# Sums of q for batch 4 added up on GpSimd, and seven products that begin ahead of their mixes, in an attention and MLP kernel

## The chip, the cores and the metric

The kernel runs on one core of a Trainium2 chip. The metric is the device time of the whole program in microseconds (us). The engines are named as the profile names them: PE is TensorE, DVE is VectorE, ACT is ScalarE, POOL is GpSimd, and SP is the engine whose queue issues most of the DMAs.

## The reference, cut to what matters

There are 8 batches of 8 heads, 576 tokens and 64 dimensions per head, and an MLP of width 2048 behind the attention.

```python
q_lm = q.reshape(B, H, m, S // m, D).mean(axis=3)      # m = 32 landmarks, 18 tokens each
k_lm = k.reshape(B, H, m, S // m, D).mean(axis=3)
A  = sm(q, k_lm); Bm = sm(q_lm, k_lm); C = sm(q_lm, k)
Z  = Bm.transpose(0, 1, 3, 2) / (norm1(Bm) * norminf(Bm) + 1e-06)
for _ in range(6):
    Z = 2 * Z - Z @ Bm @ Z
x = A @ Z @ C @ v                                       # heads side by side: 576 x 512 per batch
xn = (x - mean) / sqrt(var + 1e-06) * g_ln
out = x + maximum(xn @ w_ch1, 0) @ w_ch2
```

The landmarks are means over 18 tokens. The kernel works with sums in their place and puts the division into the scale of the exponentials. A tile of q or k holds four heads of a batch; each of its 128 partitions holds nine consecutive tokens of two heads (`[128, 2, 9, 64]`), so a landmark is the sum over the nine slots of a partition and over two neighbouring partitions.

## The kernel before, in words

The batches run as a pipeline in the sets (0), (1), (2), (3, 4), (5, 6) and (7). Class `Coming` (L971) prepares a set: `next_load` issues the loads, `next_cast` turns each tile to fp16 (`cast`, L1105), `next_job` runs the DVE steps (a transposition `turn`, and a step that brings the sums into landmark form), and `attention2` (L1263) follows. In a set of two batches the tiles are k0, k1, q0, q1 of the first batch, then k2, k3, q2, q3 of the second.

The nine slots are summed in one of three ways, picked for each tile where `sets` is built (L1848): on DVE (`add_up`, reductions of the transposed tile), on POOL right behind the cast (four additions of 512, 256, 128 and 128 columns, L1130 to L1138, into a small tile `s16` that DVE turns in `turn_sums`), or on PE (`total`, L1043). `total` runs nine products against the constant `pairs16`, which adds neighbouring partitions and spreads the result over the rows; the nine add up in one PSUM bank. ACT copies it to `tot`, and `turn_totals` turns that on DVE into the tile `lm` of landmarks. In set (3, 4), k0 and k1 go by DVE, q0 and q1 by POOL, and k2, k3, q2, q3 (batch 4) by PE.

A cast runs on POOL, or on ACT if, at the moment it is placed, the kernel's own clock says that POOL is busy and ACT is free (`helps`, L1913).

For each batch the attention ends with `normalize` (L653): PE sums the heads (`psd`), ACT takes logarithm and exponential (`lns`), POOL multiplies `ea` by it. The batch's rows (`zcbd` by `ea`, into x) and the first MLP layer (`chunk`, L1564: `psh` from `m16` and `ea`) both read the normalized `ea`. ReLU, mostly on ACT, writes the hidden tile `hT`.

The second MLP layer multiplies `hT` by `w2_16`. For batches 4 to 7 it is `seven_products` (L1738), a Strassen form for a 512 x 512 block: seven products in place of eight, of mixed operands. The mixes of the weights (`w2mix`, t1 to t4) are made once by POOL (`mix_w2`), those of the hidden tile (s1, s2 and the rewritten h21) for each batch by DVE (`mix_ahead`). The first two products, h11 by w11 and h12 by w21, read no mixes. As the code stands, the generator first waits until all mixes of the batch are placed, and then begins with those two.

All engines execute in program order. This order is written out by hand in `ORDER` (L1853): a list of letters and counts that says which stream places its next step. 0 is the attentions, 1 the totals, 2 the first layers, 4 the second layers, J a DVE job, M a measurement of a block, X a mix of the hidden tile, W one of the weights, K a cast, L a load. A step that isn't possible at its turn is placed as soon as it is. Changing one entry can change every queue behind it.

Of the kernel before, what the change touches and what calls it, by code (L numbers as in the profile page):

```python
# [16 lines left out]
P = 128  # L17
# [3 lines left out]
def kernel(  # L21
# [20 lines left out]
    MCH = HID // P  # L42
    U = H // 4
    NJ = 9
# [17 lines left out]
    NEVER = 1e12  # L62
# [4 lines left out]
    parted, mixed_, parted_w1 = {}, set(), set()  # L67
# [219 lines left out]
    clock = Clock()  # L287
# [245 lines left out]
    asm = Ring(name="asm", bufs=2)  # L533
# [435 lines left out]
                    block_done(j)  # L969

    class Coming:  # L971
        def __init__(self, bs, by_dve, by_pe=()):
            self.bs, self.by_dve, self.by_pe = bs, by_dve, by_pe
            self.units = [(b, u) for b in bs for u in range(U)]
            pairs = [(w, w + 1) for w in range(0, len(self.units), 2)]
            self.parts = [(nm, w) for pair in pairs for nm in ("k", "q") for w in pair]
            self.parts += [("v", w) for w in range(len(self.units))]
            n = len(self.units)
            self.loads, self.casts = list(range(3 * n)), list(range(3 * n))
            self.jobs = []  # L980
            for i, (nm, w) in enumerate(self.parts[:2 * n]):
                self.jobs.append((self.turn, i))
                if nm + str(w) in by_pe:
                    self.jobs.append((self.turn_totals, i))
                elif nm + str(w) in by_dve:
                    self.jobs += [(self.add_up, i, 0), (self.add_up, i, 1)]
                else:
                    self.jobs.append((self.turn_sums, i))
            self.stg, self.n16, self.sums, self.xT, self.part, self.lm = {}, {}, {}, {}, {}, {}
            self.totals, self.uses, self.lm_tiles = {}, {}, {}  # L990
# [14 lines left out]
        def cast_ready(self):  # L1005
            i = self.casts[0]
            if i not in self.stg:
                return NEVER
            nm, w = self.parts[i]
            if nm == "v":  # L1010
                b = self.units[w][0]
                if b - 2 not in multiplied:
                    return NEVER
                return max(clock.at(self.stg[i]), clock.idle(natv_buf[b % NV]))
            return max(clock.at(self.stg[i]), nat.next("nat"),
                       asm.next("s16") if self.by_pool(nm, w) else 0.0)

        def by_pool(self, nm, w):
            return nm + str(w) not in self.by_dve and nm + str(w) not in self.by_pe
# [13 lines left out]

        def total_ready(self, i):
            if self.bs not in PAIRED:
                if i not in self.n16:
                    return NEVER
                return max(clock.at(self.n16[i]), banks.next(), asm.next("tot"))
            if i not in self.n16 or i + 1 not in self.n16:
                return NEVER  # L1040
            return max(clock.at(self.n16[i], self.n16[i + 1]), banks.next(2), asm.next("tot", 2))

        def total(self, i):  # L1043

            if self.bs not in PAIRED:
                psl = banks.take([P, 2, D])
                for j in range(NJ):
                    MM(psl, pairs16[:].rearrange("p e h l -> p (e h l)"), self.n16[i][:, :, j, :],
                       start=(j == 0), stop=(j == NJ - 1))
                self.totals[i] = asm.pin(asm.tile([P, 2, D], FP16, name="tot", tag="tot", bufs=4 if PAIRED else 2))  # L1050
                scalar.copy(self.totals[i][:], psl)
                self.used(i)
                return
            psl = [banks.take([P, 2, D]) for _ in range(2)]
            for j in range(NJ):
                for x in range(2):
                    for e in range(2):
                        rows, cb = ds(64 * e, 64), 64 * (e ^ x)
                        MM(psl[x][ds(cb, 64)], pairs16[rows, e, :, :].rearrange("p h l -> p (h l)"),
                           self.n16[i + x][rows, :, j, :], rb=64 * e, cb=cb,  # L1060
                           start=(j == 0), stop=(j == NJ - 1), skip=True)
            for x in range(2):
                t = asm.pin(asm.tile([P, 2, D], FP16, name="tot", tag="tot", bufs=4))
                self.totals[i + x] = t
                for to, of in (((slice(0, P), slice(0, P)),) if x == 0 else
                               ((slice(0, 64), slice(64, P)), (slice(64, P), slice(0, 64)))):
                    scalar.copy(t[to], psl[x][of])
                self.used(i + x)
# [36 lines left out]
        def cast(self, i, by_act=False, part=None):  # L1105
# [19 lines left out]
            else:  # L1125
                pool.tensor_copy(out=t[:], in_=stg[:])
            self.n16[i] = nat.pin(t)
            self.uses[i] = 2 if nm + str(w) in self.by_pe else 1
            if self.by_pool(nm, w):
                s = asum.tile([P, 2, 4, D], FP32, name="asum", tag="asum")  # L1130
                s16 = asm.tile([P, 2, D], FP16, name="s16", tag="s16", bufs=4)
                self.sums[i] = asm.pin(s16)
                for o, x, y in ((s[:], t[:, :, 0:4, :], t[:, :, 4:8, :]),
                                (s[:, :, 0:2, :], s[:, :, 0:2, :], s[:, :, 2:4, :]),
                                (s[:, :, 0, :], s[:, :, 0, :], s[:, :, 1, :]),
                                (s16[:], s[:, :, 0, :], t[:, :, 8, :])):
                    with nc.allow_low_precision("sums are rounded once, to fp16"):
                        pool.tensor_tensor(out=o, in0=x, in1=y, op=ALU.add)  # L1138
# [597 lines left out]
            h_mixed.add(b)  # L1736

    def seven_products(b):  # L1738

        while b not in h_mixed:  # L1740
            yield lambda: NEVER if b not in h_mixed and len(w2_mix) < 6 else 0.0
            if b not in h_mixed:
                if hTs[b].name not in mixed_:
                    yield lambda: clock.at_key(hTs[b][:, MCH - 1, 0:P])
                mix_ahead()
        t1, t2, t3, t4, s1, s2 = [t[:] for t in w2_mix]
        h11, h12, h21, h22 = parts_of(b)
        j0 = 9 * (b // 2) + 4 * (b % 2)

# [35 lines left out]
        yield from finished(b)  # L1785
        if not early:
            add(0, 0, a)
        yield from product(a, s2, t2, False)
        add(0, 0, e)
        banks.release(e[0])  # L1790
# [52 lines left out]
    def scaled_by_pe():  # L1843
# [2 lines left out]
        dve.tensor_scalar(out=g_sb[:], in0=psg[:], scalar1=UP, scalar2=None, op0=ALU.mult)  # L1846

    sets = [Coming((1,), (), ("k0", "k1", "q0", "q1"))]  # L1848
    sets += [Coming(bs, [f"k{w}" for w in range(U * len(bs))] if bs != (3, 4) else ["k0", "k1"], ("k2", "k3", "q2", "q3") if bs == (3, 4) else ()) for bs in ((2,), (3, 4), (5, 6), (7,))]

    begun_first = [0]

    ORDER = (  # L1853
# [19 lines left out]
    ).split()  # L1873
    JOB, MEASURE, CENTER, MIX, MIX_W2, CAST, LOAD, MEANS = range(5, 13)

# [175 lines left out]
```

## Time and profile before

| | us |
|---|---|
| median of 3 runs | 260.68 (260.4 to 261.2) |
| profiled execution, its own time | 260.16 |
| profiled execution, span from first to last instruction | 258.4 |
| PE matmul busy in the span | 250.6 |
| DVE busy | 203.8 |
| ACT busy | 174.0 |
| POOL busy | 141.0, nearly all of it before 166 us |

The page divides the span over 40 slices of 6.46 us. POOL is nearly always at work from slice 4 to slice 25 and rests for most of the last third; ACT is between 4 and 9 tenths busy, DVE mostly 8 or 9. In the chain of work that ended last, PE has 92% of the span. A busy PE isn't a PE at its peak: matmuls overlap in the pipeline, and the profile models their ends. The distance between the starts of two groups in the chain of waits, or in the timeline, says more than the mean duration of one matmul, which also holds the way through the array.

### The profile page before, as it was taken

The numbers are of one execution on the slowest core, as the hardware profiler recorded it, in microseconds if no ns is written. First come the engines' busy times: TensorE is split into PE (matmuls) and PEld (weight loads), VectorE is DVE, ScalarE is ACT, GpSimd is POOL, SyncE is SP. The second block draws the span as 40 slices with busy tenths as digits, with TensorE's granted clock in tenths as the row PEclk, the third lists the DMA queues.
The fourth block names the chain that finished last, engine by engine and source line by source line (L and its number), as shares of the span: only waits on it lengthen the run. The fifth ranks groups of instructions, "written<-read, shape, count | busy, mean of one in ns | idle before, by whom it ended". The sixth has DMA issues, their size and how long they took to land.

```text
span 258.4 us, 8623 instructions
## 1 busy us (share of the span) xinstructions
PE 250.6 (97%) x3551; PEld 168.4 (65%) x3551; DVE 203.8 (79%) x464; ACT 174.0 (67%) x335; POOL 141.0 (55%) x166
## 2 busy tenths in 40 slices
PE   6889999999999999999999999999999999999994
PEld 6645754556455664546655466688878875888883
DVE  2768966999988989997998865968398878697861
ACT  2788976468858986389987668647888737786000
POOL 5188789999992889689899997300000006000000
PEclk9999999999999999999999999999999999999999
DMA  6999999997976895858943101300240034100705
GB/s 252 373 398 371 394 405 393 365 335 235 352 212 185 299 351 157 257 169 225 365 129 79 46 5 40 81 3 1 68 99 1 3 81 94 32 3 3 162 20 186
DMA packets 23119, 46.70 MB, mean 181 GB/s; under 512 B 2980, under 2 KB 3240, under 8 KB 23080
## 3 DMA queue, kind: packets, MB, share of 16 engines
q1 hardware_dynamic: 22600, 45.50, 54.4%
q10 hardware_dynamic: 480, 0.66, 0.8%
q8 instruction: 28, 0.46, 0.7%
q14 instruction: 11, 0.09, 0.1%
HBM read 36.70 MB, written 9.44 MB: 179 GB/s over the span
## 4 chain that ended last, share of the span: by engine, by line
PE 92%; DMA 2%; DVE 2%; POOL 1%; issue 0%; ACT 0%; SPq 0%; DVEq 0%; POOLq 0%
PE bank L345 60%; PE psh L345 25%; DMA stg<-in_q_dram 2%; PE pscv L345 2%; PE psd L345 2%; PE psea L345 1%; PE psec L345 1%; PE psr L345 1%; POOL w L339 1%; PE pszt L345 0%; DVE st L339 0%; SPq L354 0%; DVE m L339 0%; PE pszc L345 0%; DVE nat L339 0%
## 5 line engine op out<-in xcount | busy, mean ns | idle before, releaser
L345 PE MATMUL bank<-w,hT 128*128 128x512 f16 (+3 forms) x528 | 111.6, 335 | 0.0
L339 ACT ACTIVATE hT<-psh 128x576 f16<-128x576 f32 x122 | 76.9, 655 | 26.3 <-PE psh L345 25.1
L345 PE MATMUL psh<-ea,m 128*128 128x288 f16 x512 | 80.6, 286 | 0.3 <-DVE m L339 0.2
L345 PEld LDWEIGHTS <-hT 128*128 128x128 f16 x656 | 60.4, 98 | 28.1 <-issue 4.3
L345 PEld LDWEIGHTS <-m 128*128 128x128 f16 x512 | 49.4, 98 | 19.5 <-issue 0.7
L339 DVE SCALAR_TENSOR_TENSOR xblk<-bank,rstd,xblk 128x256 f32<-128x256 f32 (+2 forms) x77 | 39.0, 539 | 19.4 <-PE bank L345 18.7
L339 POOL TENSOR_TENSOR ea<-ea,lns 128x576 f16<-128x576 f16 x16 | 20.9, 1318 | 55.8 <-ACT lns L339 55.8
L339 POOL CAST nat<-stg 128x1152 f16<-128x1152 f32 x27 | 31.2, 1165 | 9.4 <-DVE xT L339 4.7
L339 DVE BATCH_NORM_STATS2 six<-xblk 128x6 f32<-128x512 f32 x36 | 24.3, 676 | 0.5 <-ACT xblk L339 0.4
L339 POOL CAST natv<-stg 128x1152 f16<-128x1152 f32 (+1 forms) x17 | 19.4, 1165 | 8.5 <-DMA stg<-in_v_dram 8.4
L339 DVE STREAM_TRANSPOSE xT<-nat 128x576 uint32<-128x576 uint32 x28 | 21.2, 758 | 0.0
L339 DVE SCALAR_TENSOR_TENSOR st<-st,bank 128x128 f16<-128x128 f16 (+3 forms) x36 | 13.2, 367 | 8.2 <-PE bank L345 8.0
L339 ACT ACTIVATE lns<-psd 128x576 f32<-128x576 f32 x16 | 10.3, 647 | 11.7 <-PE psd L345 11.6
L345 PE MATMUL bank<-w2mix 128*128 128x256 f16 x128 | 17.8, 273 | 0.0
L345 PE MATMUL bank<-w2mix,hT 128*128 128x256 f16 x128 | 17.2, 273 | 0.0
L339 DVE TENSOR_REDUCE part<-xT 128x32 f16<-128x576 f16 x20 | 14.5, 738 | 0.1
L339 ACT CAST m<-bank 128x512 f16<-128x512 f32 x20 | 11.3, 589 | 4.1 <-PE bank L345 3.9
L339 ACT COPY xblk<-bank 128x512 f32<-128x512 f32 (+1 forms) x22 | 12.9, 598 | 1.2 <-PE bank L345 1.0
L345 PEld LDWEIGHTS <-w2mix 128*128 128x128 f16 x128 | 12.4, 98 | 2.0
L345 PEld LDWEIGHTS <-st 32*32 32x32 f16 (+1 forms) x380 | 7.0, 90 | 9.3 <-DVE st L339 4.3
L339 POOL TENSOR_TENSOR asum<-asum 128x256 f32<-128x256 f32 (+1 forms) x20 | 12.2, 609 | 1.6
L339 ACT ACTIVATE ea<-psea 128x576 f16<-128x576 f32 x14 | 8.3, 648 | 6.9 <-PE psea L345 6.9
(132 smaller groups left out, 370.1 us busy)
## 6 DMA issues: line engine op xcount, KB each, us to landing
stg<-in_q_dram SPq DMA_DIRECT2D x16, 576.0 KB, 6.8
stg<-in_k_dram SPq DMA_DIRECT2D x15, 576.0 KB, 5.2
out_dram<-xblk SPq DMA_DIRECT2D x66, 128.0 KB, 2.4
wstg<-in_moe_w_ch_dram SPq DMA_DIRECT2D x16, 512.0 KB, 7.1
stg<-in_v_dram SPq DMA_DIRECT2D x5, 576.0 KB, 6.9
stg<-in_v_dram SPq DMA_DIRECT2D x40, 72.0 KB, 2.7
stg<-in_v_dram SPq DMA_DIRECT2D x6, 288.0 KB, 5.5
stg<-in_v_dram SPq DMA_DIRECT2D x12, 144.0 KB, 2.9
```

The source lines that it names most:

```text
L339: return lambda *args, **kw: keep(getattr(self.engine, op)(*args, **kw))
L345: keep(nc.tensor.matmul(o, l, r, start=start, stop=stop, tile_position=(rb, cb), skip_group_check=(skip or cb != 0)))
```

## The change

Class `Coming` takes one more list, `added`. A tile in `by_pe` that is also in `added` is cast as before, then summed by POOL with the same four additions as q0 and q1, and `total` multiplies the sum once by `pairs16` in place of the nine slots. The tile's own fp16 copy then has one reader, the transposition, in place of two. The list names q2 and q3 of set (3, 4), the two q tiles of batch 4; k2 and k3 keep their nine products each.

In `seven_products` the loop that waits for the mixes moves from the head of the generator to the place in front of the third product, the first one that reads a mix.

`ORDER` is written anew. The first difference on PE is at about 65 us of the span. From there the order of fillers, casts, jobs, mixes, measurements and loads shifts by a few places, at many places; the kinds and numbers of the instructions stay the same but for those named here and the choice between ACT and DVE, or ACT and POOL, for a few copies.

```diff
-            self.bs, self.by_dve, self.by_pe = bs, by_dve, by_pe
+            self.bs, self.by_dve, self.by_pe, self.added = bs, by_dve, by_pe, added
...
+        def summed(self, nm, w):
+            return self.by_pool(nm, w) or nm + str(w) in self.added
...
             if self.bs not in PAIRED:
+                if i in self.sums:
+                    return max(clock.at(self.sums[i]), banks.next(), asm.next("tot"))
                 if i not in self.n16:
                     return NEVER
...
                 psl = banks.take([P, 2, D])
-                for j in range(NJ):
-                    MM(psl, pairs16[:].rearrange("p e h l -> p (e h l)"), self.n16[i][:, :, j, :],
-                       start=(j == 0), stop=(j == NJ - 1))
+                added = self.sums.pop(i, None)
+                of = ([self.n16[i][:, :, j, :] for j in range(NJ)] if added is None
+                      else [added[:]])
+                for j, x in enumerate(of):
+                    MM(psl, pairs16[:].rearrange("p e h l -> p (e h l)"), x,
+                       start=(j == 0), stop=(j == len(of) - 1))
...
-            self.uses[i] = 2 if nm + str(w) in self.by_pe else 1
-            if self.by_pool(nm, w):
+            self.uses[i] = 2 if nm + str(w) in self.by_pe and nm + str(w) not in self.added else 1
+            if self.summed(nm, w):
...
     def seven_products(b):
-
-        while b not in h_mixed:
-            yield lambda: NEVER if b not in h_mixed and len(w2_mix) < 6 else 0.0
-            if b not in h_mixed:
-                if hTs[b].name not in mixed_:
-                    yield lambda: clock.at_key(hTs[b][:, MCH - 1, 0:P])
-                mix_ahead()
-        t1, t2, t3, t4, s1, s2 = [t[:] for t in w2_mix]
         h11, h12, h21, h22 = parts_of(b)
...
         if not early:
             add(0, 0, a)
+        while b not in h_mixed:
+            yield lambda: NEVER if b not in h_mixed and len(w2_mix) < 6 else 0.0
+            if b not in h_mixed:
+                if hTs[b].name not in mixed_:
+                    yield lambda: clock.at_key(hTs[b][:, MCH - 1, 0:P])
+                mix_ahead()
+        t1, t2, t3, t4, s1, s2 = [t[:] for t in w2_mix]
         yield from product(a, s2, t2, False)
...
+    sets += [Coming(bs, ..., ("k2", "k3", "q2", "q3") if bs == (3, 4) else (),
+                    ("q2", "q3") if bs == (3, 4) else ()) for bs in ((2,), (3, 4), (5, 6), (7,))]
```

More of the change, by code (lines that the diff above doesn't have):

```diff
@@ L971, with __init__ @@
     class Coming:
-        def __init__(self, bs, by_dve, by_pe=()):
-            self.bs, self.by_dve, self.by_pe = bs, by_dve, by_pe
+        def __init__(self, bs, by_dve, by_pe=(), added=()):
+            self.bs, self.by_dve, self.by_pe, self.added = bs, by_dve, by_pe, added
             self.units = [(b, u) for b in bs for u in range(U)]
@@ L1015, in cast_ready @@
             return max(clock.at(self.stg[i]), nat.next("nat"),
-                       asm.next("s16") if self.by_pool(nm, w) else 0.0)
+                       asm.next("s16") if self.summed(nm, w) else 0.0)
+        def summed(self, nm, w):
+            return self.by_pool(nm, w) or nm + str(w) in self.added
         def by_pool(self, nm, w):
@@ L1046, in total @@
                 psl = banks.take([P, 2, D])
-                for j in range(NJ):
-                    MM(psl, pairs16[:].rearrange("p e h l -> p (e h l)"), self.n16[i][:, :, j, :],
-                       start=(j == 0), stop=(j == NJ - 1))
+                added = self.sums.pop(i, None)
[4 more added lines that the diff above has]
+                       start=(j == 0), stop=(j == len(of) - 1))
                 self.totals[i] = asm.pin(asm.tile([P, 2, D], FP16, name="tot", tag="tot", bufs=4 if PAIRED else 2))
                 scalar.copy(self.totals[i][:], psl)
-                self.used(i)
+                if added is None:
+                    self.used(i)
+                else:
+                    asm.unpin(added)
                 return
@@ L1848 @@
     sets = [Coming((1,), (), ("k0", "k1", "q0", "q1"))]
-    sets += [Coming(bs, [f"k{w}" for w in range(U * len(bs))] if bs != (3, 4) else ["k0", "k1"], ("k2", "k3", "q2", "q3") if bs == (3, 4) else ()) for bs in ((2,), (3, 4), (5, 6), (7,))]
+    sets += [Coming(bs, [f"k{w}" for w in range(U * len(bs))] if bs != (3, 4) else ["k0", "k1"], ("k2", "k3", "q2", "q3") if bs == (3, 4) else (),
+                    ("q2", "q3") if bs == (3, 4) else ()) for bs in ((2,), (3, 4), (5, 6), (7,))]
     begun_first = [0]
     ORDER = (
[19 rows of a table removed]
[19 rows of a table added]
     ).split()
```

38 rows, old and new, of the table ORDER are left out of this document.

## The prediction

> **What bounds the kernel now.** I read the page's busy shares first, then the table of stretches, then the chain of waits, and last the timelines of single engines around the places that the change touches.
>
> ```profile
> span 258.4 us, 8623 instructions
> ...
> PE 250.6 (97%) x3551; PEld 168.4 (65%) x3551; DVE 203.8 (79%) x464; ACT 174.0 (67%) x335; POOL 141.0 (55%) x166
> ```
>
> ```profile
> 60.00:76.00 16.00, 16.00 (x218) 9.77 (x217) 14.80 (x37) 12.39 (x26) 15.37 (x17) 1.00 0.80 259
> 76.00:92.00 16.00, 16.00 (x157) 9.53 (x155) 14.67 (x31) 13.62 (x26) 9.99 (x9) 1.00 0.79 246
> ...
> 156.00:172.00 16.00, 16.00 (x202) 11.06 (x201) 11.93 (x24) 10.84 (x20) 6.26 (x6) 1.00 0.16 36
> 172.00:188.00 16.00, 16.00 (x221) 13.06 (x219) 10.44 (x23) 11.62 (x22) 0.00 (x0) 1.00 0.15 35
> ```
>
> The columns are the stretch, its length, then PE, PE's weight loads, DVE, ACT and POOL. PE is busy for 16.00 of 16 us in each stretch shown, and has no gap that the profile would book as a wait. The granted clock is 1.00. So in the middle of the program PE's own queue is the bound: a product taken from it shortens the end by its slot, and each new wait of PE lengthens it by its full length. POOL is nearly full from 60 to 76 us (15.37 of 16), less so from 76 to 92 (9.99): that is where the change adds to POOL.
>
> **The products that go.** In the changed program, 72 products of `nat` by `pairs16` become 54, and 2 of the sums come in: 16 fewer. Nothing else on PE differs in number.
>
> ```profile
> 92.81 0.50 PE bank L345 x9
> ...
> 107.16 1.18 PE pscv L345 x68
> ...
> 150.48 0.65 PE pscv L345 x35
> 151.36 0.65 PE pscv L345 x36
> ```
>
> The first row of the chain of waits is one of the two groups of nine that go: 0.50 / 9 = 0.056 us each, 16 x 0.056 = 0.89 us. The removed weight loads ran beside the products. The last three rows price a second, small gain of the new order: in set (5, 6) the two groups of `pscv` now stand side by side, with the step of the iteration behind them instead of between them. Side by side in set (3, 4), 72 products (4 of them not recorded) took 1.18 us, apart 2 x 0.65 = 1.30, so 0.12 us.
>
> **What POOL and ACT take over.** Four additions more for each of q2 and q3, and two casts (k3 and q2) that go from POOL to ACT.
>
> ```profile
> 65.18 1.54 POOL L339 TENSOR_TENSOR asum<-nat 128x512 f32<-128x512 f16 x1
> 66.80 1.60 POOL L339 TENSOR_TENSOR asum<-asum 128x256 f32<-128x256 f32 x2
> 68.47 0.49 POOL L339 TENSOR_TENSOR s<-asum,nat 128x128 f16<-128x128 f32 x1
> ...
> 70.13 1.16 POOL L339 TENSOR_TENSOR asum<-nat 128x512 f32<-128x512 f16 x1
> 71.37 1.26 POOL L339 TENSOR_TENSOR asum<-asum 128x256 f32<-128x256 f32 x2
> 72.71 0.43 POOL L339 TENSOR_TENSOR s<-asum,nat 128x128 f16<-128x128 f32 x1
> 73.08 1.15 POOL L339 CAST nat<-stg 128x1152 f16<-128x1152 f32 x1
> 74.18 1.29 POOL L339 TENSOR_TENSOR ea<-ea,lns 128x576 f16<-128x576 f16 x1
> 75.41 1.15 POOL L339 CAST nat<-stg 128x1152 f16<-128x1152 f32 x1
> 76.52 1.80 POOL L339 TENSOR_TENSOR ea<-ea,lns 128x576 f16<-128x576 f16 x1
> 82.98 1.14 POOL L339 CAST nat<-stg 128x1152 f16<-128x1152 f32 x1 [4.67 <-DVE xT L339]
> 84.07 4.49 POOL L339 CAST natv<-stg 128x1152 f16<-128x1152 f32 x4
> ```
>
> One set of additions takes from 70.13 to 73.14, 3.0 us, or from 65.18 to 68.96, 3.8 us. Two sets are 6.0 to 7.6 us, less the two casts of 1.15 that leave: 3.7 to 5.3 us more work for POOL. Between 73.08 and 84.07 POOL stands idle for 4.67 us, for a transposition that frees a tile; the changed DVE order has that transposition about 2 us sooner, between the centering steps. So the four casts of v begin near 84 to 85 us as before, and what follows on POOL's queue (loads' buffers, the casts of set (5, 6)) moves by less than 1 us. Those casts feed stages that lie tens of us later; I cost this at nothing. If the cover were gone, the first to be late would be the loads that wait for a freed buffer, not PE.
>
> ```profile
> 68.06 1.21 ACT L339 CAST nat<-stg 128x1152 f16<-128x1152 f32 x1
> 69.84 1.19 ACT L339 ACTIVATE ea<-psea 128x576 f16<-128x576 f32 x2 [0.57 <-PE psea L345]
> 72.47 0.65 ACT L339 ACTIVATE lns<-psd 128x576 f32<-128x576 f32 x1 [1.44 <-PE psd L345]
> 73.16 0.68 ACT L339 ACTIVATE lns<-lns 128x576 f32<-128x576 f32 x1
> 73.75 0.25 ACT L339 CAST tot<-bank 128x128 f16<-128x128 f32 x1
> 74.36 0.65 ACT L339 ACTIVATE lns<-psd 128x576 f32<-128x576 f32 x1 [0.37 <-PE psd L345]
> 75.05 0.68 ACT L339 ACTIVATE lns<-lns 128x576 f32<-128x576 f32 x1
> ```
>
> On ACT a cast takes 1.21 us. The first moved one falls into the idle 1.44 us before 72.47. The second comes behind `tot`, from 74.00 to 75.21, and pushes the second pair of `lns` from 74.36 to 75.2, its end from 75.73 to 76.6.
>
> **The new wait.** On POOL the changed order of batch 2's normalization is: first `ea`, four additions of q2, second `ea`. Behind the second `ea` wait batch 2's first rows and its first `psh` on PE, and all else in PE's queue.
>
> ```profile
> 76.48 0.68 DVE L339 TENSOR_TENSOR w<-w,less 128x1024 f16<-128x1024 f16 x1
> ...
> 78.40 1.89 DVE L339 TENSOR_TENSOR w<-w,less 128x1024 f16<-128x1024 f16 x3
> ```
>
> ```profile
> 78.19 1.47 PE L345 MATMUL bank<-w,hT 128*128 128x512 f16 x6
> 79.50 0.38 PE L345 MATMUL bank<-zcbd,ea 128*128 128x256 f16 x2
> ```
>
> q2's cast ends at 75.21 on ACT, so the additions run from there: 3.0 us if undisturbed, 3.8 if disturbed, to 78.2 or 79.0. The second `ea` then takes 1.29 to 1.80 us, to 79.5 or 80.8, where it ended at 78.32 before. PE gets to the second product of `zcbd` by `ea` at 79.50, plus one filler more in the changed order (1.47 us stand for six with the last one's tail; 79.50 - 78.19 = 1.31, so 0.22 each), plus half of the pair (0.11): 79.8. The wait is between 0 and 1.0 us. I take 0.3: one centering step on DVE (76.48) meets the additions and costs what it cost `ea` before (1.80 - 1.29 = 0.5), the next ones come behind `zcbd` in the changed order, so 75.2 + 3.0 + 0.5 + 1.3 = 80.0, and 0.1 for the hand-over.
>
> The row of 76.52 is the trace's evidence that such a step holds POOL: 1.80 against 1.29 us for the same multiplication, with a DVE step of 0.68 us beside it. The Trainium skill, "SBUF — State Buffer", section "Who interferes with whom", says that a VectorE instruction with two SBUF inputs and a GpSimd instruction that reads SBUF exclude each other for a whole instruction. The 0.5 us agree with most of that. By it the second `ea` would meet a step as well: it is the third rival below.
>
> **The later mixes.** The moved loop lets h11 by w11 of batch 4 begin before the mixes are placed; since PE had no idle time there, it only changes which product is the filler. It is worth nothing by itself. But the second half of s2 moves on DVE.
>
> ```profile
> 161.92 1.29 DVE L339 TENSOR_TENSOR w2mix<-w2mix,hT 128x1024 f16<-128x1024 f16 x2
> 163.31 1.42 DVE L339 TENSOR_TENSOR zcbd<-pszc,heads 128x256 f16<-128x256 f32 x4
> ...
> 166.12 0.68 DVE L339 COPY xblk<-psr 128x512 f32<-128x512 f32 x1
> ...
> 167.92 0.87 DVE L339 SCALAR_TENSOR_TENSOR xblk<-bank,rstd,xblk 128x256 f32<-128x256 f32 x2
> ```
>
> ```profile
> 169.62 0.49 PE L345 MATMUL bank<-w2mix 128*128 128x256 f16 x3
> ```
>
> For batch 4 it now stands behind `zcbd`, two copies and the first pair of additions into x: 166.12 + 0.60 + 0.80 + 0.65 puts its end at 168.2. PE's first product with s2 began at 169.62 and reads the second half only four products later. That leaves 1.4 us and more; I cost it at nothing, with 0 and 0.65 (half of 1.29) as ends.
>
> **The sum.** 260.16 - 0.89 - 0.12 + 0.30 = 259.45 for the profiled execution; the median of the runs lies 0.52 above that execution, so 259.97, or 260.0.
>
> **Rivals.**
> 1. No wait arises: the additions run undisturbed and the second `ea` is there by 79.5. For it: the four additions at 70.13 ran beside DVE work in 3.0 us. Against it: the step at 76.48. 259.6, and a little less if the new order saves more changes of tile size on PE.
> 2. The mixes become the bound, the slower side. In batches 4, 6 and 7 the changed DVE queue has copies or additions into x between the halves of s2. If DVE runs later than reckoned by more than the 1.4 us, PE stands in front of the fifth product with s2, each time for about half a mix, 0.65 us. Three times: 260.0 + 1.95 = 261.9. For it: DVE is the second busiest engine (203.8 us) and works in order, so a late PSUM bank holds the mixes behind it. Against it: 10.44 to 11.93 of 16 us busy in these stretches.
> 3. POOL is held for whole DVE instructions twice, in the additions and in the second `ea`: 75.2 + 3.0 + 0.68 + 1.29 + 0.68 + 0.1 = 80.95, a wait of 1.15, and the time is 260.16 - 1.01 + 1.15 + 0.52 = 260.8. The Trainium skill's page named above would have it so; the 0.5 us of the trace speak for somewhat less.
> 4. The freed 0.89 us turn into waits elsewhere in the new order, in a stage that waits for DVE's iteration steps rather than for PE: 260.7 or so. Against it: the stretches without any idle time.
>
> **How the numbers follow.** I give the forecast 0.36, rival 1 0.26, rival 2 0.20, rival 3 0.10, rival 4 0.08. What a measurement of this kernel can tell from no change is 0.3%, 0.78 us: below 259.90 is faster, above 261.46 slower. The forecast's own range is 259.6 to 260.4, some four tenths of it below 259.90: 0.14, with rival 1 0.40 for faster. Slower is rival 2 (0.20) and a tail of rivals 3 and 4 where two costs meet (0.05): 0.25. The rest, 0.35, is within. The range of 259.0 to 261.9 holds all of the forecast and rivals 1, 3 and 4 and half of rival 2.
>
> **What would show it.** In the changed profile: 56 products with `pairs16`, two of them of `s`, and 16 fewer products in all; twelve sets of additions on POOL and three casts of `nat` on ACT; POOL's second `ea` of batch 2 ending near 80.0 and a gap of some 0.3 us on PE before `zcbd` by `ea`; from there PE ahead of the old trace by about 0.6 us to the end; no wait of PE for `w2mix` by DVE. The prediction is wrong if PE shows idle time in front of products with s2, if the second `ea` ends after 81, or if the end moves by more than 1.2 us without a wait at either place.

## The result and the profile after

| | before | changed |
|---|---|---|
| median of 10 runs each, us | 260.93 | 259.38 |
| lowest to highest, us | 259.84 to 261.56 | 258.93 to 260.32 |
| profiled execution, own time, us | 260.16 | 259.04 |
| its span, us | 258.4 | 257.3 |

The ratio is 0.9946, with a 95% interval of 0.9927 to 0.9965: faster by some 1.4 us, 0.9 to 1.9. The profiled executions differ by 1.12 us. The page of the changed kernel, its span and busy times and one group of GpSimd:

```profile
span 257.3 us, 8602 instructions
...
PE 249.9 (97%) x3535; PEld 168.0 (65%) x3535; DVE 205.4 (80%) x467; ACT 175.5 (68%) x334; POOL 144.2 (56%) x172
...
L339 POOL TENSOR_TENSOR asum<-nat 128x512 f32<-128x512 f16 x12 | 14.8, 1236 | 0.9
```

PE has 16 instructions fewer (3551 to 3535), and GpSimd makes twelve sets of additions instead of ten. The stretch of the new wait in the changed kernel, in the columns of before (PE, weight loads, DVE, ACT, POOL, clock):

```profile
76.00:92.00 16.00, 16.00 (x159) 9.50 (x157) 15.40 (x30) 14.40 (x28) 14.15 (x16) 1.00 0.74 237
```

PE is as full as it was. POOL goes from 9.99 to 14.15 us of 16 in this stretch, and DVE from 14.67 to 15.40: the spare time that the change draws on is nearly used up. The timelines of the changed kernel at the place of the new wait, first GpSimd's:

```profile
75.31 1.15 POOL L339 TENSOR_TENSOR asum<-nat 128x512 f32<-128x512 f16 x1
76.55 1.59 POOL L339 TENSOR_TENSOR asum<-asum 128x256 f32<-128x256 f32 x2
78.22 0.43 POOL L339 TENSOR_TENSOR s<-asum,nat 128x128 f16<-128x128 f32 x1
78.60 1.29 POOL L339 TENSOR_TENSOR ea<-ea,lns 128x576 f16<-128x576 f16 x1
81.20 1.51 POOL L339 CAST nat<-stg 128x1152 f16<-128x1152 f32 x1 [1.30 <-DVE xT L339]
...
86.06 4.47 POOL L339 CAST natv<-stg 128x1152 f16<-128x1152 f32 x4
```

ScalarE's:

```profile
75.75 0.68 ACT L339 ACTIVATE lns<-lns 128x576 f32<-128x576 f32 x1
```

And TensorE's, with four rows further on:

```profile
79.81 0.43 PE L345 MATMUL bank<-zcbd,ea 128*128 128x256 f16 x2
80.07 1.14 PE L345 MATMUL psh<-ea,m 128*128 128x288 f16 x8
...
99.70 0.22 PE L345 MATMUL bank<-st,bones 128*128 128x128 f16 x1
...
149.69 1.25 PE L345 MATMUL pscv<-natv,ecT 64*64 64x130 f16 x72
...
151.10 0.42 PE L345 MATMUL psd<-ea,bones 128*128 128x288 f16 x2
...
224.28 0.51 PE L345 MATMUL psr<-zcbd,ea 64*32 64x128 f16 x32
```

The second `ea` of batch 2 ends at 78.60 + 1.29 = 79.89. PE begins the pair that needs it at 79.81 and reaches the next product 0.26 us later, where two slots take 0.22. So 0.04 us of waiting are left of the 0.30 forecast. The rows of before that the later four answer to, from TensorE's timeline:

```profile
100.30 0.22 PE L345 MATMUL bank<-st,bones 128*128 128x128 f16 x1
...
150.41 0.72 PE L345 MATMUL pscv<-natv,ecT 64*64 64x130 f16 x36
...
151.94 0.42 PE L345 MATMUL psd<-ea,bones 128*128 128x288 f16 x2
...
225.29 0.51 PE L345 MATMUL psr<-zcbd,ea 64*32 64x128 f16 x32
```

PE's queue is the same in both kernels up to 71.5 us (not 65, as the section on the change has it), and in that stretch the changed kernel is 0.09 us late: a `part` by `spread` begins at 63.44 against 63.35. Behind the two sums, at 100 us, its lead is 0.60 us; at `pscv` it is 0.72, at `psd` at 151 us 0.84, at the last `psr` 1.01, and at the end of the span 1.1. Ahead of the first three of these rows PE has done the same products in both kernels but for the 16; ahead of the last `psr` the changed kernel has done one product by `w2mix` more (0.11 us), so in equal work it leads by 1.12 there. From `pscv` to `psd` it takes 151.10 - 149.69 = 1.41 us against 151.94 - 150.41 = 1.53: the two groups side by side are worth 0.12.

### The profile page after: what moved, and what is told of

The parts are those of the page before. It is cut to its first block, busy times and chain, and to the rows that moved or that the text cites. A ratio compares the mean times of both kernels' runs of the same rounds, so it can differ in the third digit from the quotient of the medians.

```text
span 257.3 us, 8602 instructions
## 1 busy us (share of the span) xinstructions
PE 249.9 (97%) x3535; PEld 168.0 (65%) x3535; DVE 205.4 (80%) x467; ACT 175.5 (68%) x334; POOL 144.2 (56%) x172
## 4 chain that ended last, share of the span: by engine, by line
PE 93%; DMA 3%; DVE 2%; ACT 0%; issue 0%; SPq 0%; DVEq 0%
PE bank L345 60%; PE psh L345 25%; DMA stg<-in_q_dram 3%; PE pscv L345 2%; PE psd L345 2%; PE psea L345 1%; PE psec L345 1%; PE psr L345 1%; PE pszt L345 0%; SPq L354 0%; PE pszc L345 0%; DVE nat L339 0%; DVE st L339 0%; PE pst L349 0%; ACT hT L339 0%
## 5 line engine op out<-in xcount | busy, mean ns | idle before, releaser
L339 ACT ACTIVATE hT<-psh 128x576 f16<-128x576 f32 x121 | 76.6, 652 | 26.1 <-PE psh L345 24.3
L339 POOL CAST nat<-stg 128x1152 f16<-128x1152 f32 x25 | 29.2, 1182 | 5.1 <-DMA stg<-in_q_dram 2.4
L345 PE MATMUL bank<-w2mix,hT 128*128 128x256 f16 x128 | 17.8, 273 | 0.0
L339 POOL TENSOR_TENSOR asum<-asum 128x256 f32<-128x256 f32 (+1 forms) x24 | 14.9, 620 | 1.9
L339 POOL TENSOR_TENSOR asum<-nat 128x512 f32<-128x512 f16 x12 | 14.8, 1236 | 0.9
L339 ACT COPY xblk<-bank 128x512 f32<-128x512 f32 (+1 forms) x21 | 12.2, 591 | 1.2 <-PE bank L345 1.0
```

The costliest lines, as they stand in the source:

```text
L339: return lambda *args, **kw: keep(getattr(self.engine, op)(*args, **kw))
L345: keep(nc.tensor.matmul(o, l, r, start=start, stop=stop, tile_position=(rb, cb), skip_group_check=(skip or cb != 0)))
```

## The experiments

Ten kernels were run, one of them twice. Each ratio is to the kernel before on the same chip in the same session, so ratios compare better than medians. The changed kernel stands at 0.9946.

**Is it the products?** The changed kernel, with eight products by a block of zeros behind each of the two products that spread a sum: PE gets its 16 slots back, all else stays.

```diff
+                for j in range(len(of), NJ):
+                    tc.keep_in_program_order(nc.tensor.matmul(psl, pairs16..., zeros[:, ds(2 * P, P)]..., start=False, ...))
```

> The changed kernel, with 8 products of a block of zeros behind each of the two products of the sums, so that PE issues as many products as before; all other queues keep their order. My theory (the gain is PE slots): about 0.9 us slower than the changed kernel, 16 x 0.056 us, so a ratio to the kernel before near 0.998, and in the trace PE later by 0.9 us from 94 us to the end. Rival (the new order of the queues brings the gain, the products were worth nothing): no change against the changed kernel, 0.995.

Measured: 260.82 us, ratio 0.9991 (0.9975 to 1.0006). Its TensorE timeline around one of the two, and two rows further on:

```profile
92.94 0.22 PE L345 MATMUL bank<-s,pairs 128*128 128x128 f16 x1
93.00 0.61 PE L1059 MATMUL bank<-zeros,pairs 128*128 128x128 f16 x8
93.44 0.59 PE L345 MATMUL bank<-w,hT 128*128 128x512 f16 x2
...
152.21 0.42 PE L345 MATMUL psd<-ea,bones 128*128 128x288 f16 x2
...
225.39 0.51 PE L345 MATMUL psr<-zcbd,ea 64*32 64x128 f16 x32
```

The eight take 93.44 - 93.00 = 0.44 us, so 0.88 in all, and the time rises by 0.45% or 1.2 us, which agrees with 0.88 within the intervals. With the products back, no difference from the kernel before can be measured, so the gain needs their slots; the interval leaves room for up to 0.65 us that the order brings by itself. The traces show about 0.5: from the rows at 100 us to the end, behind the products, the changed kernel's lead grows from 0.60 to 1.1. Part of that is seen here too: the last two rows lie 73.18 us apart, as they do in the changed kernel (224.28 - 151.10); in the kernel before it is 225.29 - 151.94 = 73.35, with one product less in between.

**The new order without the additions.** The list of q2 and q3 to be added is left empty: order and loop as changed, nine products for each sum on PE, nothing of q2 and q3 added on GpSimd.

```diff
-                    ("q2", "q3") if bs == (3, 4) else ()) for bs in ((2,), (3, 4), (5, 6), (7,))]
+                    ()) for bs in ((2,), (3, 4), (5, 6), (7,))]
```

> The changed kernel with an empty list of added tiles: the new order and the moved loop stay, q2 and q3 are summed by nine products on PE again, GpSimd's eight additions are gone. My theory: the additions were hidden, so this is as fast as the kernel with 16 products of zeros, ratio near 0.998; what is left against the kernel before is what the order brings by itself, 0.2 to 0.5 us. Rival (the additions cost PE a wait between the two normalizations of batch 2): faster than the kernel with zero products by 0.3 us. Rival (the order is the whole gain): 0.995.

Measured: 261.27 us, ratio 1.0011 (0.9994 to 1.0029). The order without the additions gives nothing that can be measured; the 0.2% of gain that was expected of it didn't come. The trace shows where it goes. In this kernel an iteration step stands between the two groups of `pscv` again, so the 0.12 us are missing. Where the changed kernel has q2's additions, the second `ea` now runs beside the centering step on DVE, which takes 1.77 us (from 77.48) instead of 1.25, and PE loses 0.41 us against the changed kernel between 78 and 84 us. It loses 0.60 more between 153 and 164 us, which wasn't followed up. So taking the additions out moves other queues too, and this kernel isn't the order alone.

**The additions without the new order.** The kernel before, its order and its loop, with q2 and q3 added on GpSimd (class `Coming` as changed).

```diff
-    sets += [Coming(bs, ..., ("k2", "k3", "q2", "q3") if bs == (3, 4) else ()) for bs in ...]
+    sets += [Coming(bs, ..., ("k2", "k3", "q2", "q3") if bs == (3, 4) else (),
+                    ("q2", "q3") if bs == (3, 4) else ()) for bs in ...]
```

> The kernel before, its old order and old place of the loop, with q2 and q3 added up by GpSimd. Here GpSimd also casts q2 itself between the two multiplications of batch 2. My theory: 0.9 us less on PE, but the second multiplication ends at 80.9 to 82.2 us while PE arrives at 79.8, a wait of 1.1 to 2.4 us, so 0.2 to 1.5 us slower than the kernel before, ratio 1.001 to 1.006. Rival (a wait of PE there is made good later): ratio 0.9966.

Measured: 264.25 us, ratio 1.0134 (1.0106 to 1.0162), more loss than either bound. Its GpSimd timeline, then TensorE's:

```profile
75.46 1.15 POOL L339 CAST nat<-stg 128x1152 f16<-128x1152 f32 x1
76.68 1.53 POOL L339 TENSOR_TENSOR asum<-nat 128x512 f32<-128x512 f16 x1
...
80.67 1.72 POOL L339 TENSOR_TENSOR ea<-ea,lns 128x576 f16<-128x576 f16 x1
```

```profile
82.45 0.28 PE L345 MATMUL bank<-zcbd,ea 128*128 128x256 f16 x1 [2.65 <-POOL ea L339]
```

In the old order q2's cast stands on GpSimd between the first `ea` and the additions, and the second `ea` ends at 82.39 instead of 79.89. The bracket gives the idle time and its releaser: PE waits 2.65 us for it, more than the products save. Of the 2.50 us by which that `ea` is later, 1.37 lie ahead of the additions (76.68 against 75.31), where the cast is; in the other 1.13 the additions and the `ea` themselves run longer. So the cast on ScalarE makes more than half of the room for the additions. The profiled execution lost 4.5 us against the changed kernel's span; what isn't this wait lies in waits of 0.2 to 0.3 us and in later stretches, and wasn't followed up.

**The loop moved alone.** The kernel before, with only the loop that places the mixes moved behind the first product of `seven_products`.

```diff
     def seven_products(b):
-        while b not in h_mixed:
-            ...
-        t1, t2, t3, t4, s1, s2 = [t[:] for t in w2_mix]
...
             add(0, 0, a)
+        while b not in h_mixed:
+            ...
+        t1, t2, t3, t4, s1, s2 = [t[:] for t in w2_mix]
         yield from product(a, s2, t2, False)
```

> The kernel before with nothing but the wait for the mixes moved in front of the third product. My theory: PE has no idle time there, so nothing changes, ratio 0.999 to 1.001. Rival (the early begin is where the gain beyond 0.9 us comes from): ratio 0.997 to 0.998.

Measured: 266.04 us, ratio 1.0178 (1.0143 to 1.0213). That refutes what was expected. Its DVE timeline, TensorE's, and two stretches:

```profile
196.79 0.69 DVE L339 CAST m<-psm 128x512 f16<-128x512 f32 x1 [3.14 <-PE psm L345]
...
197.99 1.28 DVE L339 TENSOR_TENSOR w2mix<-hT 128x1024 f16<-128x1024 f16 x2
199.19 1.28 DVE L339 TENSOR_TENSOR w2mix<-w2mix,hT 128x1024 f16<-128x1024 f16 x2
```

```profile
199.93 2.07 PE L345 MATMUL bank<-w2mix 128*128 128x256 f16 x10 [2.90 <-DVE w2mix L339]
```

```profile
198.00:200.00 2.00, 0.07 (x1) 0.07 (x2) 2.00 (x5) 0.69 (x2) 0.00 (x0) 1.00 0.00 0
200.00:202.00 2.00, 2.00 (x11) 1.28 (x12) 2.00 (x4) 0.00 (x0) 0.00 (x0) 0.56 0.01 4
```

With the loop behind the product, the old order issues the mixes of batch 5 behind a cast of `m`, and that cast waits 3.14 us for PE. When PE is through, it needs the mixes and stands still for 2.90 us. This is close to the prediction's second rival, but PE stands in front of the first product with s2 instead of the fifth; of the two orders that were run with the loop moved, the changed one avoids it. Behind the wait the granted clock is 0.56: the 22 products from 199.93 to 204.12 take 4.19 us, and an estimate from their spacing at full clock in the changed kernel (0.11 and 0.12 us each) is 2.5. Together 2.9 + 1.7 = 4.6 us, as much as the ratio says. The clock is taken up below.

**The loop moved back in the changed kernel.** The same edit the other way round.

> The changed kernel with the wait for the mixes back at the head of the seven products, the new order and the additions kept; the mixes of batches 4 to 7 then stand elsewhere on VectorE. My theory: within 0.3 us of the changed kernel, ratio 0.994 to 0.996. Rival (the moved loop saves PE waits behind 160 us): 0.5 us or more slower, 0.997 or above.

Measured: 260.95 us, ratio 1.0014 (0.9992 to 1.0037): the gain is gone. The timelines of DVE, ScalarE and TensorE in this kernel, and DVE's in the changed one:

```profile
218.40 0.87 DVE L339 TENSOR_TENSOR w2mix<-w2mix,hT 128x1024 f16<-128x1024 f16 x1
219.19 2.12 DVE L339 TENSOR_TENSOR hT<-hT 128x1024 f16<-128x1024 f16 x2
221.24 0.68 DVE L339 COPY xblk<-psr 128x512 f32<-128x512 f32 x1
```

```profile
221.94 0.58 ACT L339 COPY xblk<-psr 128x512 f32<-128x512 f32 x1 [1.27 <-DVE xblk L339]
```

```profile
222.58 0.65 PE L345 MATMUL psh<-ea,m 128*128 128x288 f16 x4 [0.67 <-ACT xblk L339]
```

```profile
218.46 0.68 DVE L339 COPY xblk<-psr 128x512 f32<-128x512 f32 x1
...
219.84 0.68 DVE L339 TENSOR_TENSOR w2mix<-w2mix,hT 128x1024 f16<-128x1024 f16 x1
```

With the loop at the head, the mixes come ahead of the copy out of `psr` on DVE (221.24 instead of 218.46), ScalarE's copy waits for DVE's, and PE waits 0.67 us for the bank. By the ratios the loss is 0.7%, 1.8 us. The span of the profiled execution is 2.5 us longer than the changed kernel's, but 1.1 of that is there at 71 us, ahead of anything that the edit touches: 0.42 at 41 us, from the waits for the first inputs; 0.43 more at this row of PE,

```profile
48.68 1.02 PE L345 MATMUL psh<-ea,m 128*128 128x288 f16 x7 [0.27 <-POOL ea L339]
```

which waits for an `ea` that GpSimd does behind casts of weights, and four of these casts had waited 0.20 to 0.26 us for their DMAs; and 0.25 by 71 us, behind a centering step on DVE that took 0.93 us instead of 0.67. The instructions up to there are the same in both. Of the 1.4 us behind 71 us the wait at 222.58 explains 0.83 from start to start and one at 243.86 another 0.22; the rest wasn't followed up. So the gain needs both: the slots, and a place for the mixes that keeps DVE's copies in time.

**More sums on GpSimd.** k2 and k3 are added there as well, 16 more products off PE.

```diff
-                    ("q2", "q3") if bs == (3, 4) else ()) ...
+                    ("k2", "k3", "q2", "q3") if bs == (3, 4) else ()) ...
```

> The changed kernel with k2 and k3 of batch 4 in the list as well: 16 products fewer on PE, 0.9 us, but two more sets of additions on GpSimd, 6 us, ahead of both multiplications of batch 2. My theory: the second multiplication ends near 82.5 us, PE waits 2.5 to 3.5 us, so the end comes 1.6 to 2.6 us later than that of the changed kernel, ratio 1.001 to 1.005. Rival (GpSimd's additions are free, as they were for q): 0.9 us faster, 0.991.

Measured: 264.31 us, ratio 1.0122 (1.0081 to 1.0163), worse than expected. TensorE's timeline:

```profile
76.51 0.27 PE L345 MATMUL bank<-s,pairs 128*128 128x128 f16 x1 [3.05 <-POOL s L339]
```

Here PE waits for a sum itself. 0.9 us of products saved cost 3.05 us of waiting, and behind it the granted clock is 0.57 to 0.58 from 76 to 80 us, which the expectation hadn't reckoned with. GpSimd has no more room at this place.

**How much later may the second `ea` be?** Two further additions of 512 columns on GpSimd between q2's sum and that `ea`; nothing reads their result.

```diff
+                if nm + str(w) == "q2" and nm + str(w) in self.added:
+                    for _ in range(2):
+                        tc.keep_in_program_order(nc.gpsimd.tensor_tensor(
+                            out=s[:], in0=t[:, :, 0:4, :], in1=t[:, :, 4:8, :], op=ALU.add))
                 s16 = asm.tile([P, 2, D], FP16, name="s16", tag="s16", bufs=4)
```

> The changed kernel with two more additions of 512 columns on GpSimd (their result is not read) between the sum of q2 and the second multiplication of batch 2, 2 x 1.2 us. My theory (in this stretch a wait of PE goes through to the end in full): the second multiplication ends near 82.3 us, PE waits about 2.3 us there, and the end comes 2.0 to 2.5 us later than that of the changed kernel, ratio to the kernel before near 1.003. Rival (PE makes the wait good later, since other engines then run ahead): under 1 us later.

Measured: 263.81 us, ratio 1.0104 (1.0064 to 1.0143), some 4.1 us over the changed kernel instead of 2.0 to 2.5. Its timelines and two stretches:

```profile
78.79 2.72 POOL L1152 TENSOR_TENSOR asum<-nat 128x512 f32<-128x512 f16 x2
81.47 1.73 POOL L339 TENSOR_TENSOR ea<-ea,lns 128x576 f16<-128x576 f16 x1
```

```profile
83.25 0.40 PE L345 MATMUL bank<-zcbd,ea 128*128 128x256 f16 x1 [3.11 <-POOL ea L339]
83.44 2.13 PE L345 MATMUL psh<-ea,m 128*128 128x288 f16 x8
```

```profile
82.00:84.00 2.00, 0.75 (x4) 0.51 (x5) 2.00 (x4) 0.31 (x1) 2.00 (x2) 0.62 0.73 200
84.00:86.00 2.00, 2.00 (x10) 1.29 (x9) 1.85 (x4) 1.32 (x3) 1.91 (x2) 0.52 0.46 124
```

Two reasons. GpSimd's additions and the `ea` behind them meet DVE's work and take 2.72 + 1.73 us instead of 2.3 + 1.29, so PE's wait is 3.11 us. And behind it PE is slow: the eight `psh` take 2.13 us where the changed kernel's take 1.14, at a granted clock of 0.52. Was it the length of the wait or its after-effect? Four more runs.

The same kernel once more:

> The kernel with two further additions on GpSimd once more, for a comparison on the same chip. Both theories: 263.5 to 264.0, ratio 1.010 to 1.012. Theory A adds that the executions fall into two groups, those in which the mean granted clock is 0.992 to 0.994 and those at 1.000, some 1.3 us apart; by theory B the clock doesn't sort them.

Measured: 263.96 us, ratio 1.0119 (1.0083 to 1.0154). In five of six runs the mean granted clock was 0.991 to 0.994 and the time 263.89 to 265.35 us; in the sixth it was 1.000 and the time 262.19. The runs of the first series divide the same way: three at 0.992 to 0.994 took 263.68 to 264.36 us, one at 1.000 took 262.35. The profiled execution here is the one at full clock, TensorE's timeline:

```profile
83.07 0.28 PE L345 MATMUL bank<-zcbd,ea 128*128 128x256 f16 x1 [3.11 <-POOL ea L339]
83.19 1.14 PE L345 MATMUL psh<-ea,m 128*128 128x288 f16 x8
```

The wait is 3.11 us again, but the `psh` behind it take 1.14. So the same wait costs more when the clock falls behind it, and whether it falls differs from run to run. How much more: 1.28 us by the two profiled executions (the same work, from this product to the next `w` by `zt`, takes 88.50 - 83.25 = 5.25 us in the one and 87.04 - 83.07 = 3.97 in the other), some 1.7 by the medians, with only two runs at full clock.

One further addition instead of two:

> The changed kernel with one further addition of 512 columns on GpSimd between q2's sum and the second ea of batch 2 (its result is used by nothing). With two of them, PE idled 3.1 us in front of zcbd by ea, and its granted clock then stood at 0.52 to 0.62 for some 4 us. Theory A (the loss is the length of the wait, and a further loss comes only where a wait is so long that the clock falls): the second ea ends 1.2 to 1.7 us later than in the changed kernel (79.9), near 81.1 to 81.6, PE idles 1.3 to 1.8 us, the granted clock stays 1.00, and the time is 260.7 to 261.2, ratio 1.000 to 1.003. Theory B (each us of that wait costs about 1.4 us whatever its length, as 4.5 us for 3.1 would have it, because work behind it is late too): 261.4 to 262.0, ratio 1.003 to 1.005.

Measured: 261.34 us, ratio 1.001 (0.999 to 1.003), which is 0.6% or 1.7 us over the changed kernel. TensorE's timeline:

```profile
81.93 0.28 PE L345 MATMUL bank<-zcbd,ea 128*128 128x256 f16 x1 [1.55 <-POOL ea L339]
```

A wait of 1.55 us costs its own length, the clock stays at 0.997 to 1.000 in all ten runs: theory A.

Two further additions, and 24 products by zero on PE where it waits:

```diff
                     MM(psy[:, ts(u, 4 * D)], ea[U * i + u][:, ds(at, P)], ...)
+                    for _ in range(24 if (b, t0, u) == (2, 0, 0) else 0):
+                        tc.keep_in_program_order(nc.tensor.matmul(
+                            psy[:, 0:P], zeros[:, 0:P], zeros[:, ds(2 * P, P)], start=False, ...))
```

> The kernel with two further additions on GpSimd, and on PE 24 products by zero behind the first product of zcbd by ea of batch 2, where PE waits (24 x 0.056 = 1.3 us of work that adds zero to a bank). Theory A (part of the loss is the fallen clock): PE's idle time shrinks from 3.1 to about 1.8 us, the granted clock stays 1.00, and although PE does more, the time falls by 1 to 1.3 us against the same kernel without the products: near 262.6, ratio 1.006. Theory B (the clock has nothing to do with it): the products lie inside the wait and the time stays at 263.8, ratio 1.010 to 1.012.

Measured: 263.40 us, ratio 1.0093 (1.0063 to 1.0124). TensorE's timeline:

```profile
81.08 1.50 PE L966 MATMUL bank<-zeros 128*128 128x128 f16 x24
84.35 0.28 PE L345 MATMUL bank<-zcbd,ea 128*128 128x256 f16 x1 [1.77 <-POOL ea L339]
```

The idle time shrinks to 1.77 us, and the clock is 0.999 to 1.000 in all six runs, where it had fallen in eight of ten without the products. The time fell by 0.6 us only, not by 1 to 1.3, and the intervals overlap. The profiled execution reached the `zcbd` pair 1.28 us later than the one above (80.97 against 79.69) and finished its span 1.3 us later; those 1.3 us lie ahead of the edit, half of them in a wait of 0.65 us for `ea` at 48.70, the place where the kernel with the loop moved back had lost time too. On the clock the test is clear, on the time it is not.

One addition less, the second of q2's four (its sums lack the slices j = 2, 3, 6 and 7):

> The changed kernel without the second of q2's four additions (leaves the slices j = 2, 3, 6, 7 out of q2's sums). The second ea of batch 2 is there 0.7 us sooner, near 79.2. By the prediction's term of 0.30 us for PE's wait: 0.3 us of gain in the stretch from 77 to 90 us, 259.1. By the changed kernel's trace, where PE arrives as the second ea ends: no more than 0.05 to 0.1 us, 259.3. The times can hardly tell these two apart; PE's rows from 78 to 90 us can. A ratio over 0.998 would say that the place isn't what bounds, and that something else depends on it.

Measured: 259.56 us, ratio 0.9941 (0.9918 to 0.9964), the changed kernel's. GpSimd's timeline and TensorE's:

```profile
77.99 1.28 POOL L339 TENSOR_TENSOR ea<-ea,lns 128x576 f16<-128x576 f16 x1
```

```profile
79.99 0.38 PE L345 MATMUL bank<-zcbd,ea 128*128 128x256 f16 x2
80.21 1.14 PE L345 MATMUL psh<-ea,m 128*128 128x288 f16 x8
```

The second `ea` ends at 79.27, 0.7 us ahead of PE, and the pair takes 0.22 us instead of 0.26. An `ea` that comes sooner buys 0.04 us, one that comes 1.5 us later costs all of it: the changed kernel uses the spare time of GpSimd to within a tenth of a microsecond.

## Why the prediction was right, and what it mis-sized

**The bound and the products (0.89).** Right. PE stays full in every stretch shown, and giving its 16 slots back (0.88 us) leaves no gain that can be measured. The fourth rival, by which the freed time would turn into waits elsewhere, came about in small: right behind the second sum a group of products (those with `lm`, then `psec`) takes 0.72 us from 93.21, where it took 0.57 before and takes 0.57 with zero products. So 0.15 of the 0.89 us were lost again at once, in gaps too short for the profile to book.

**The groups of `pscv` (0.12).** Right to the hundredth: 1.41 against 1.53 us from `pscv` to `psd`.

**The new wait (0.30).** This is the mis-sized term: it measured 0.04. Its steps held up well. The second `lns` pair ended at 76.43 (76.6 forecast), the additions took 75.31 to 78.65, and the second `ea` ended at 79.89 (80.0). PE reached the product that needs it at 79.92 rather than 79.8, since it was already 0.09 us later at 63 us in this execution, and the hand-over had been added on top. A difference of two ends was taken where each was good to 0.1 us. Its upper bound of 1.0 was sound: in other orders this wait was 1.55 to 3.11 us.

**GpSimd's meeting with DVE.** Right in that they met, not in who lost most: the centering step on DVE took 1.25 us (from 76.57) instead of 0.68, the pair of additions beside it 1.59 instead of 1.26, and the `ea` behind ran undisturbed. The third rival, two meetings at full price, didn't come about; in the kernels with further additions the `ea` did meet DVE and took 1.73 us.

**What POOL and ACT take over, at nothing.** Right for the end. But the cover was thinner than written: POOL's 4.67 us of idle time became 1.30, and the casts of v began at 86.06, 2 us later than before and not "near 84 to 85". Nothing on PE waited for them.

**The moved loop, "worth nothing by itself".** This step was wrong as a rule. Since the loop issues the mixes on DVE's queue, its place decides what stands ahead of what there: alone in the old order it costs 1.78%, and taken back in the new order it gives up the gain. It came out as nothing only because order and loop had been changed together. The margin of the later mixes was indeed there: the second half of s2 ended at 168.47 (168.2 forecast), and from 50 us on the profile books no wait to any PE row of the changed kernel.

**The sum.** 259.45 was forecast for the profiled execution, 259.04 measured; 260.0 for the median, 259.38 measured. The forecast gain of 0.71 us is smaller than the measured one, 1.12 by the profiled executions and 1.4 (0.9 to 1.9) by all runs. By 151 us the lead was to be 0.71 and is 0.84: with 0.04 for the wait, and with the 0.09 us by which this execution was late at 63 us, the same terms give 0.88. That they come so close is partly luck, for 0.15 us were lost at `psec` and 0.12 gained between 100 us (lead 0.60) and `pscv` (0.72), and the prediction had neither. Another 0.26 us come behind 151 us, where it had nothing. In equal work they lie ahead of the last `psr`, and there they are in the kernel with zero products too, so they belong to the new order or the loop; which move gives them wasn't separated. In all, the traces put some 0.7 us of the gain on the products and some 0.5 on the order and the loop, of which the prediction named 0.12.

**The chances.** Faster had the largest share, 0.40, and is what came. The first rival, no wait, at 259.6 "and a little less if the new order saves more changes of tile size on PE", describes the result best. It had the second largest chance, and what separated it from the forecast were 0.2 us between two ends. The prediction's last sign of being wrong, an end that moves by more than 1.2 us without a wait at either place, is a close call: it is 1.12 us for the profiled executions, and 1.4 by the runs.

## What to carry to other kernels

Where one engine's queue is full, a part taken from it is worth its slots only if what replaces it arrives before that engine does: reckon the arrival of both to a tenth of a microsecond, and look up what else stands in the other engine's queue. A statement that issues work on another engine's queue is not neutral when it is moved within one engine's code; compare that queue's order ahead of judging it. A wait of a few microseconds on TensorE can cost more than itself, so look at the granted clock in the stretch behind it. Two executions can differ by 1 us ahead of the place that an edit touches, so compare rows in front of it too, and only rows behind equal work.

## What the hardware showed that was not expected

The granted clock fell to 0.52 to 0.62 for about 4 us behind a single idle time of PE of 3.11 us (one profiled execution; in another, with the same 3.11 us, it stayed at 1.00), to 0.57 behind 3.05 us, and to 0.56 behind 2.90 us. Behind the profiled waits of 2.65, 1.77 and 1.55 us it stayed at 1.00 (though two of the six executions of the kernel with 2.65 had a mean clock of 0.994). With the 3.11 us wait, the eight runs at a mean clock of 0.991 to 0.994 took 263.68 to 265.35 us, the two at 1.000 took 262.19 and 262.35. The Trainium skill, "TensorE: Matmul & The Clock Gate", section "What's actually happening", says that the clock drops to half after at least one idle window of about 3.4 us and that the window runs freely. That chance decides agrees with these runs; the length does not, as 2.90 us of idle time in the profile were enough here.

The DVE step that met GpSimd's addition is the other. The centering step began at 76.57, 0.02 us behind GpSimd's pair of additions (0.63 us each when alone), and its 1.25 us are its own 0.68 and nearly one addition. DVE's timeline in the changed kernel:

```profile
76.57 1.25 DVE L339 TENSOR_TENSOR w<-w,less 128x1024 f16<-128x1024 f16 x1
```

By the Trainium skill, "SBUF — State Buffer", section "Who interferes with whom", the one that issues first holds the shared port for its whole instruction. The two rows agree on who waits: before, the step had begun 0.04 us ahead of GpSimd's `ea` and GpSimd lost 0.5 us; here GpSimd was first and DVE lost 0.57. The rows don't show a whole instruction lost each time: 0.5 us is less than the step's 0.68, and GpSimd's pair of additions lost 0.33.
